# A fourth set of exp buffers, and third readings that ride in ScalarE-only PV steps

## The chip, the cores and the metric

The kernel runs on one core of one Trainium2 chip. The metric is the device time of one execution in microseconds; each number for a kernel is the median of several runs, all of them in the fast state.

## The reference, cut to what matters

One sequence of 2048 rows of 640 features goes through a layer norm. The result feeds an attention with 32 query heads of width 20 that share one key and one value head, and beside it a dense layer with SiLU. Everything is added to the input.

```
xn = _layernorm(x, axis=-1)
q = (xn @ wq) as 32 heads of 20;  k = xn @ wk;  v = xn @ wv        # one k, one v
p = softmax((q . k) * 20 ** -0.5);  o = p @ v
return x + o @ wo + silu(xn @ w1) @ w2
```

The exponentials are the mass: 32 heads x 2048 x 2048 scores, each of which must pass ScalarE or VectorE.

## The kernel before: the parts that matter

The program is written by a planner in Python: it keeps a model of each engine's clock, picks for each engine what runs next, and emits five fixed instruction lists tied by semaphores. The constants at its head (priorities, limits on backlog) steer the plan; a changed constant changes the order of instructions, not only their number.

Work goes in 688 steps. A step takes three heads ("units") and 128 keys: an S step makes the three score blocks (128 keys x 512 queries) in three PSUM banks; two such sets of banks alternate. ScalarE reads two or all three blocks with Exp. In a "dv" step VectorE takes the third block: it clamps it to integers (p1), whose bits, read as bf16, are a coarse exponential. Two shifted copies (Y) of the same bits make the second and third reading, whose weighted sum corrects the coarse one. The PV step multiplies the exponentials with V in four 32-wide column tiles of one PSUM bank: two heads of ScalarE, the first and the second reading of VectorE's head. The tiles are then full, so the third readings, collected over up to three dv steps, get a PV pass of their own.

```
NZ = 3          # sets of Z/Y buffers
ZB = 3          # dv steps that share a set
PV_PRESS = 12   # PV is urgent when more than NBLK - PV_PRESS = 19 exp blocks wait
DVE_TH = 3.0    # VectorE gets a block while its backlog is below this
U_PRIO = 0.9;  X_PRIO = 1.6     # p1 has 1.0; lower goes first
...
    def flush_z(self):               # after ZB dv steps (2 in the last two groups)
        zs = self.zset
        self.zset = (self.zset + 1) % NZ
        ...                          # two Y copies of the whole set on VectorE
        while ts and hosts and len(ts) % 3 == 1:
            ...                      # a lone third reading may ride in a ScalarE-only step
        while ts:
            part = ts[:3]            # else up to three make a pass of their own
            ts = ts[3:]
...
        # dummy products where PE would stand still
        if room < 0.08 or self.busy_share(now) > FILL_BELOW:
            return None
```

A set of Z/Y is written again NZ flushes later. Before that, all PV steps that read it must have run. The planner knows this, and orders every engine's list so that it holds.

The softmax here doesn't subtract the row's maximum and nothing guards it: scores larger than these inputs give would overflow.

## Time and profile before

| | before |
|---|---|
| time, median | 749.66 us (749.35 to 750.24, 4 runs) |
| span of the profiled run | 747.3 us |
| dv steps (VectorE blocks) | 603 of 688 |
| passes of third readings alone | 217, and no riders |
| dummy matmuls on PE | 147 (145 with a matmul record in the trace) |

The line is of the view of one source line; it gives the smallest, median and largest duration and then the first and last start.

```profile
L748 PEld LDWEIGHTS psall<-sbt x2048: 90/91/113, 16.4 to 734.2; 32*128 32x128 bf16 x187
```

The last score starts at 734.2 us; 13.1 us of the span are left for what comes after it.

### The profile page before, as it was taken

What the parts mean: (1) busy time and instruction counts of PE and PEld (TensorE: products, weight loads), DVE (VectorE), ACT (ScalarE), POOL (GpSimd) and SP (SyncE); (2) the same over time, 40 slices, a digit from 0 to 9 for tenths busy, and PEclk for the clock granted to TensorE, in tenths of its full rate; (3) what the DMA queues carried; (4) which work ended last, traced back from release to release, by engine and by line L of the source; (5) the groups of instructions that cost most, each with busy time, mean ns of one, the idle gap of its engine ahead of it and who ended that gap; (6) DMA issues with size and microseconds to landing.
All of it is one profiled execution on the core that took longest, in us unless ns stands there. A gap on an engine that the chain in (4) does not pass through costs nothing.

```text
span 747.3 us, 17758 instructions
## 1 busy us (share of the span) xinstructions
PE 713.0 (95%) x6724; PEld 230.7 (31%) x6779; DVE 709.2 (95%) x1390; ACT 709.3 (95%) x780; POOL 105.6 (14%) x280
## 2 busy tenths in 40 slices
PE   8889999999999999999999999999999999999996
PEld 4332222233323322223333332222333332223342
DVE  7889999999999999999999999999999999999987
ACT  7879999999999999999999999999999999999952
POOL 5421111010111111111011111101011100101100
PEclk9999999999999999999999999999999999999999
DMA  6570000000012211000002211000002110000011
GB/s 188 148 264 16 21 15 15 18 13 15 16 23 54 58 33 22 10 8 8 9 9 43 58 40 34 14 8 8 9 8 51 42 47 8 15 9 8 9 36 36
DMA packets 55962, 27.06 MB, mean 36 GB/s; under 512 B 43686, under 2 KB 55238, under 8 KB 55878
## 3 DMA queue, kind: packets, MB, share of 16 engines
q1 hardware_dynamic: 54566, 25.87, 13.4%
q8 instruction: 55, 0.90, 0.5%
q10 hardware_dynamic: 1312, 0.05, 0.1%
q14 instruction: 29, 0.24, 0.1%
HBM read 11.36 MB, written 2.62 MB: 19 GB/s over the span
## 4 chain that ended last, share of the span: by engine, by line
PE 51%; ACT 22%; DVE 15%; issue 6%; DMA 2%; POOL 2%; SPq 0%; DVEq 0%; ACTq 0%; POOLq 0%
ACT sbt L766 20%; PE psall L748 17%; PE psall L827 17%; PE psall L1112 8%; DVE sbt L780 7%; DVE sbt L839 4%; PE psall L1050 3%; ACT sbt L1058 3%; PE psall L1117 3%; DMA sbt<-sbt 2%; PE psall L1016 2%; PE psall L672 1%; DVE sbt L938 1%; DVE sbt L1023 0%; DVE sbt L1063 0%
## 5 line engine op out<-in xcount | busy, mean ns | idle before, releaser
L766 ACT ACTIVATE sbt<-psall 128x1024 bf16<-128x1024 f32 (+2 forms) x688 | 676.8, 1130 | 21.1 <-PE psall L748 15.7
L780 DVE TENSOR_SCALAR sbt<-psall 128x512 int16<-128x512 f32 x603 | 403.0, 683 | 15.0 <-PE psall L748 11.9
L748 PE MATMUL psall<-sbt 32*128 32x512 bf16 x2048 | 269.0, 385 | 14.1 <-ACT sbt L766 9.0
L827 PE MATMUL psall<-sbt 128*32 128x512 bf16 x3428 | 263.7, 384 | 1.7 <-DVE sbt L938 1.3
L839 DVE TENSOR_SCALAR sbt<-sbt 128x1536 int16<-128x1536 int16 (+2 forms) x434 | 220.0, 528 | 1.8
L748 PEld LDWEIGHTS psall<-sbt 32*128 32x128 bf16 x2048 | 68.7, 91 | 253.8 <-ACT sbt L766 123.6
L827 PEld LDWEIGHTS psall<-sbt 128*32 128x32 bf16 x3428 | 67.7, 94 | 111.5 <-issue 67.2
L908 POOL CAST sbt<-sbt 128x168 f32<-128x168 bf16 x42 | 15.2, 361 | 546.4 <-DMA sbt<-sbt 546.4
L1112 PE MATMUL psall<-sbt 128*128 128x320 bf16 x448 | 85.8, 302 | 0.1
L1050 PE MATMUL psall<-sbt 128*128 128x512 bf16 (+1 forms) x246 | 75.9, 384 | 4.6 <-issue 2.4
L1112 PEld LDWEIGHTS psall<-sbt 128*128 128x128 bf16 x448 | 34.8, 97 | 43.6 <-issue 33.0
L1063 DVE SCALAR_TENSOR_TENSOR sbt<-sbt,psall 128x512 bf16<-128x512 bf16 (+1 forms) x56 | 38.0, 679 | 3.1 <-PE psall L748 2.0
L1058 ACT ACTIVATE sbt<-psall 128x512 bf16<-128x512 f32 (+1 forms) x56 | 38.6, 689 | 0.0
L924 POOL TENSOR_TENSOR sbt<-sbt 128x240 bf16<-128x240 f32 (+2 forms) x44 | 26.7, 608 | 46.1 <-DVE sbt L915 46.1
L1117 PE MATMUL psall<-sbt 128*128 128x320 bf16 x160 | 31.3, 303 | 1.2 <-DVE sbt L1095 0.7
L1050 PEld LDWEIGHTS psall<-sbt 128*128 128x128 bf16 (+1 forms) x280 | 19.2, 98 | 41.5 <-issue 26.7
L938 DVE CAST sbt<-psall 128x512 bf16<-128x512 f32 x43 | 29.4, 683 | 1.4 <-PE psall L827 1.3
L910 POOL TENSOR_TENSOR sbt<-sbt 128x44 f32<-128x44 f32 x84 | 26.2, 312 | 6.6
L1016 PE MATMUL psall<-sbt 128*128 128x512 bf16 (+1 forms) x78 | 24.7, 384 | 2.3 <-issue 1.7
L672 PE MATMUL psall<-sbt 128*32 128x512 bf16 (+7 forms) x78 | 23.6, 353 | 0.0
L685 PE MATMUL psall<-sbt 128*128 128x512 bf16 (+4 forms) x67 | 18.2, 412 | 2.2 <-POOL sbt L1276 1.4
L1117 PEld LDWEIGHTS psall<-sbt 128*128 128x128 bf16 x160 | 12.1, 97 | 17.2 <-issue 9.7
(85 smaller groups left out, 198.6 us busy)
## 6 DMA issues: line engine op xcount, KB each, us to landing
sbt<-in_A_x_dram SPq DMA_DIRECT2D x32, 160.0 KB, 3.5
out_dram<-sbt SPq DMA_DIRECT2D x16, 160.0 KB, 1.8
sbt<-in_B_w_dram SPq DMA_DIRECT2D x5, 432.0 KB, 5.3
sbt<-sbt SPq DMA_DIRECT2D x105, 20.0 KB
sbt<-in_B_w_dram SPq DMA_DIRECT2D x13, 160.0 KB, 3.9
sbt<-sbt SPq DMA_TRANSPOSE x67, 2.4
sbt<-in_A_wo_dram SPq DMA_DIRECT2D x5, 160.0 KB, 6.2
sbt<-in_A_wq_dram SPq DMA_DIRECT2D x5, 140.0 KB, 3.7
```

Of the source, the lines that this page charges most:

```text
L748: ins = pe.matmul(self.bk(par3 + j), self.kT[r:r + SLOT, kk, kt * P:(kt + 1) * P], self.qT[r:r + SLOT, h // 4, (x // H) % 2, :], start=Tru ...
L766: return a.activation(self.E[:, b0 * QW:(b0 + na) * QW], self.ps[:, par3 * BANK:(par3 + na) * BANK], AF.Exp, scale=ACT_SCALE)
L780: return v.tensor_scalar(self.Z[:, zs, zp * QW:(zp + 1) * QW], self.bk(bb), 0.0, ZMAX, ALU.max, ALU.min)
L827: return pe.matmul(self.bk(UBANK, 0, QW, q * SLOT, (q + 1) * SLOT), self.v[:, w, kt, :], x, start=start, stop=stop, tile_position=(0, q * ...
L839: sc.new("dve", t_dve_4x(w), lambda v, k=k: v.tensor_scalar(self.Y[:, zs, k, 0:n * QW], Z, float(PH[k + 1][0]), None, ALU.add), zk, [("Y", ...
L938: return v.tensor_copy(self.U[0:rows, up, :], self.bk(UBANK, 0, QW, 0, rows))
L1016: return pe.matmul(self.bk(b, 0, QW, 0, rows), self.wq[:, k, lo:hi], self.xnT[:, k, c * QW:(c + 1) * QW], start=(k == 0), stop=(k == DC - 1))
L1050: return pe.matmul(self.bk(b, 0, QW, 0, rows), self.w1[:, k, fk * P:fk * P + rows], self.xnT[:, k, c * QW:(c + 1) * QW], start=(k == 0), s ...
L1058: sc.new("act", t_act(QW), lambda a: a.activation(t, src, AF.Tanh, scale=0.5), [("B", b)], [("tb", tp)], prio=X_PRIO, name=f"th{c}_{fk}")
L1063: sc.new("dve", t_dve_ps(QW), lambda v: v.scalar_tensor_tensor(out=self.hT[0:rows, fk, :], in0=t, scalar=1.0, in1=src, op0=ALU.add, op1=AL ...
L1112: return pe.matmul(self.bk(b, 0, 320), self.hT[0:rows, fk, i * P:(i + 1) * P], self.w2[0:rows, fk, e0:e0 + 320], start=(m == 0), stop=(m = ...
L1117: return pe.matmul(self.bk(b, 0, 320), self.oT[:, k, i * P:(i + 1) * P], self.wo[:, k, e0:e0 + 320], start=(m == 0), stop=(m == tot - 1))
```

## The change

Its intent: free enough memory for a fourth Z/Y set, so that a set may stay in use for longer, and use that freedom to carry third readings over from flush to flush. A step in which ScalarE takes all three heads leaves the fourth column tile free, and such a step can now take one third reading along. Five constants are tuned anew.

```diff
-NZ = 3
+NZ = 4
-PV_PRESS = 12
-DVE_TH = 3.0
-U_PRIO = 0.9
-X_PRIO = 1.6
+PV_PRESS = 8
+DVE_TH = 3.2
+U_PRIO = 1.1
+X_PRIO = 0.8
-DVE_FROM = 10
+DVE_FROM = 8
@@ memory
-        self.wqp = sb([P, DC, 2 * P], BF16)       # now inside oT
-        self.kv_st = sb([P, 2, DC, DH], BF16)     # now inside U
-        self.wk = sb([P, DC, P], BF16)            # now inside ost
-        self.o = sb([P, 2, 4, D], BF16)
+        self.o = sb([P, 4, D], BF16)
@@ do_S: a new ScalarE-only step takes a carried reading
+        if self.thirds and self.can_host(pv):
+            self.host(pv, self.thirds.pop(0))
@@ flush_z
-        while ts and hosts and len(ts) % 3 == 1:
-            ...
-        while ts:
-            part = ts[:3]
-            ts = ts[3:]
+            if seen and self.can_host(op) and ts:
+                self.host(op, ts.pop())
+        ...
+        self.thirds += ts
+        while len(self.thirds) >= 3 or (end and self.thirds):
+            part = self.thirds[:3]
+            self.thirds = self.thirds[3:]
```

(Cut, besides what `...` stands for: the helpers can_host and host, keys of the dependence tracking for the shared memory, one rule on banks for the v products in the start, the index c % 2 that goes with the second o buffer.)

More of the change, by code (lines that the diff above doesn't have):

```diff
@@ L379, in alloc @@
         self.U = sb([P, 2, QW], BF16)
+        self.kv_st = self.U[:, 1, 0:2 * DC * DH].rearrange("p (a c d) -> p a c d", a=2, c=DC)
         self.stk = sb([P, 64], BF16)
@@ L383, in alloc @@
         self.hT = sb([P, FC, QW], BF16)
-        self.o = sb([P, 2, 4, D], BF16)
+        self.o = sb([P, 4, D], BF16)
         self.oT = sb([P, DC, QW], BF16)
+        self.wqp = self.oT[:, :, :].rearrange("p c e -> p (c e)")[:, 0:DC * 2 * P].rearrange("p (c e) -> p c e", c=DC)
         self.tb = sb([P, 2, QW], BF16)
@@ L390, in alloc @@
         self.ost = sb([P, 3, D], BF16)
+        self.wk = self.ost[:, 2, :].rearrange("p (c e) -> p c e", c=DC)
         self.idf = self.w2[:, 4, 0:2 * P].bitcast(F32)
@@ L406, in alloc @@
         hflat = self.hT[:, :, :].rearrange("p a b -> p (a b)")
-        oflat = self.o[:, :, :, :].rearrange("p a b c -> p (a b c)")
-        self.okeys = [("o", a, h) for a in range(2) for h in range(H)]
+        oflat = self.o[:, :, :].rearrange("p b c -> p (b c)")
+        self.okeys = [("o", h) for h in range(H)]
         def xslot(n):
@@ L414, in xslot @@
                 return self.xres[:, n - self.XS, :]
-            return oflat[:, DC * D:(DC + 1) * D]
+            return oflat[:, 3 * D:4 * D]
         def xkeys(n):
@@ L459, in steps_init @@
         self.nqd = 0
+        self.thirds = []
         self.y_done = {}
@@ L475, in more, with bank_for_job @@
                 or self.cur_job is not None)
-    def bank_for_job(self):
-        if not self.started:
+    def bank_for_job(self, job=None):
+        if not self.started and (job is None or job.name[0] != "v"):
             banks = [7, 6, 5, 4, 3]
@@ L514, in job_ready @@
             return INF
-        return max(r, self.bank_for_job()[0])
+        return max(r, self.bank_for_job(job)[0])
     def s_reads(self, t, dv):
@@ L633, in step @@
                 job = cand.popleft()
-                job.bank = self.bank_for_job()[1]
+                job.bank = self.bank_for_job(job)[1]
                 self.cur_job = job
@@ L857, in flush_z @@
         first = self.zblocks[0][1]
-        tail = None
-        if self.pv_wait[-1][0].kt == KT - 1:
-            tail = self.pv_wait.pop()
+        end = self.pv_wait[-1][0].kt == KT - 1
+        tail = self.pv_wait.pop() if end else None
         seen = False
-        hosts = []
         for op, _ in self.pv_wait:
             seen = seen or op is first
-            if seen and op.after is not None and not op.after and op.kt < KT:
-                hosts.append(op)
-        while ts and hosts and len(ts) % 3 == 1:
-            th, key, kt = ts.pop()
-            op = hosts.pop()
-            op.after.append(th)
-            op.mm += 1
-            op.deps |= sc.deps_of([key], ())
-            sc.readers[key].append(op)
-        while ts:
-            part = ts[:3]
-            ts = ts[3:]
+            if seen and self.can_host(op) and ts:
+                self.host(op, ts.pop())
+        if end and self.can_host(tail[0]) and len(self.thirds + ts) % 3 == 1:
+            self.host(tail[0], ts.pop() if ts else self.thirds.pop())
+        self.thirds += ts
+        while len(self.thirds) >= 3 or (end and self.thirds):
+            part = self.thirds[:3]
+            self.thirds = self.thirds[3:]
             def fn(pe, part=part):
@@ L884, in flush_z @@
             op.mm = len(part) + len(part) // 3
-            op.kt = part[-1][2]
+            op.kt = max(x[2] for x in part)
             op.na = 0
@@ L891, in flush_z, with can_host, host @@
         self.zblocks = []
+    def can_host(self, op):
+        return op.after is not None and not op.after and op.kt < KT
+    def host(self, op, third):
+        th, key, kt = third
+        op.after.append(th)
+        op.mm += 1
+        op.deps |= self.sc.deps_of([key], ())
+        self.sc.readers[key].append(op)
     def norm_dma(self, g, rows):
@@ L919, in norm_dma @@
             h0, m = us[js[0]] % H, len(js)
-            dst = self.o[:, c % 2, :, h0 * DH:(h0 + m) * DH].rearrange("p q (i d) -> p q i d", d=DH)
+            dst = self.o[:, :, h0 * DH:(h0 + m) * DH].rearrange("p q (i d) -> p q i d", d=DH)
             src = w[:, :, js[0]:js[0] + m, 0:DH]
@@ L924, in norm_dma @@
             sc.new("pool", 0.15 + 4 * m * DH * 0.00186, lambda v, dst=dst, src=src, rb=rb: v.tensor_tensor(
-                dst, src, rb, ALU.mult), [("W", 0), ("W", 1), ("rL", up)], [("o", c % 2, h0 + i) for i in range(m)],
+                dst, src, rb, ALU.mult), [("W", 0), ("W", 1), ("rL", up)], [("o", h0 + i) for i in range(m)],
                 prio=0.5, name=f"nrm{g}").lock = True
@@ L974, in end_group @@
                 m = len(rq)
-                dst = self.o[:, c % 2, :, hh * DH:(hh + m) * DH].rearrange("p q (i d) -> p q i d", d=DH)
+                dst = self.o[:, :, hh * DH:(hh + m) * DH].rearrange("p q (i d) -> p q i d", d=DH)
                 src = xv[:, :, rq[0]:rq[0] + m, 0:DH]
@@ L979, in end_group @@
                 op.after.append(sc.new("dve", t_dve_ps(4 * m * DH), lambda v, dst=dst, src=src, rb=rb: v.tensor_tensor(
-                    dst, src, rb, ALU.mult), [("UB",), ("rL", up)], [("o", c % 2, hh + i) for i in range(m)],
+                    dst, src, rb, ALU.mult), [("UB",), ("rL", up)], [("o", hh + i) for i in range(m)],
                     prio=U_PRIO, name=f"nrm{g}"))
@@ L1005, in consume @@
                        [("B", b), ("offq",)], ks, prio=X_PRIO, name=f"qev0_{ht}")
-        reads = [("xnT", i) for i in range(4)] + [("wq", ht)]
+        reads = [("xnT", i) for i in range(4)] + [("wq", ht)] + [("oT", i) for i in range(4)]
         return Job(f"q0_{ht}", mms, reads, consume, width=QW)
@@ L1077, in try_oT @@
             op = self.sc.dma("sp", lambda q, i=i: q.dma_start_transpose(
-                self.oT[:, 0:nk, i * P:(i + 1) * P], self.o[:, c % 2, i, 0:nk * P]),
-                [("o", c % 2, h) for h in range(need)], [("oT", i), ("oTv", c, i)], nk * P * P * 2,
+                self.oT[:, 0:nk, i * P:(i + 1) * P], self.o[:, i, 0:nk * P]),
+                [("o", h) for h in range(need)], [("oT", i), ("oTv", c, i)], nk * P * P * 2,
                 sem=self.s_oT[i], name="oTd")
@@ L1089, in f @@
             def f(pe, b, i=i):
-                return pe.transpose(self.bk16(b)[:, i * P:(i + 1) * P], self.o[:, c % 2, i, k * P:(k + 1) * P],
+                return pe.transpose(self.bk16(b)[:, i * P:(i + 1) * P], self.o[:, i, k * P:(k + 1) * P],
                                     self.idb[:, :])
@@ L1096, in consume @@
                    [("B", b)], [("oT", i) for i in range(4)] + [("oTl",)], prio=X_PRIO, name="oTl")
-        reads = [("o", c % 2, h) for h in range(H)] + [("idb",)]
+        reads = [("o", h) for h in range(H)] + [("idb",)]
         return Job("oTl", mms, reads, consume, gate=lambda: self.norm_made[c] == H)
@@ L1277, in prologue @@
         pool(0.1, lambda g: g.memset(self.eps[:, :], EPS), [], [("eps",)])
-        pool(0.7, lambda g: g.memset(self.wk[:, :, :], 0.0), [], [("wk",)])
+        pool(0.7, lambda g: g.memset(self.wk[:, :, :], 0.0), [], [("wk",), ("ost", 2, 0), ("ost", 2, 1)])
         wqd = self.wqp[:, :, :].rearrange("p c (h j) -> p c h j", j=SLOT)
@@ L1281, in prologue @@
         for kk in range(2):
-            pool(0.4, lambda g, kk=kk: g.memset(wqd[:, :, 4 * kk:4 * kk + 4, DH:SLOT], 0.0), [], [("wq", kk)])
+            pool(0.4, lambda g, kk=kk: g.memset(wqd[:, :, 4 * kk:4 * kk + 4, DH:SLOT], 0.0), [],
+                 [("wq", kk)] + [("oT", i) for i in range(4)])
         iv = self.idf[:, :].rearrange("p (r j) -> p r j", j=SLOT)[:, :, DH:DH + 2]
@@ L1313, in wkrep @@
             s = self.kv_st[:, 0, :, :]
-            src = bass.AP(self.kv_st, s.offset, [list(s.ap[0]), list(s.ap[1]), [0, 4], [1, DH]])
+            src = bass.AP(self.U, s.offset, [list(s.ap[0]), list(s.ap[1]), [0, 4], [1, DH]])
             return a.activation(dst, src, AF.Copy)
@@ L1350, in mvk @@
             return [("mv", n) for n in range(a, b_)]
-        oflat = self.o[:, :, :, :].rearrange("p a b c -> p (a b c)")
+        oflat = self.o[:, :, :].rearrange("p b c -> p (b c)")
         def xa(n):
@@ L1434, in prologue @@
                     self.qT[:, ht, par, :], self.zero[:, 0:QW], self.offq[:, :], None, ALU.add),
-                    [("zero",), ("offq",)], [("qb", par, h) for h in range(4 * ht, 4 * ht + 4)],
+                    [("zero",), ("offq",), ("mv", 3)], [("qb", par, h) for h in range(4 * ht, 4 * ht + 4)],
                     prio=6.0 + par, name="qz")
@@ L1479, in consume @@
                                                                  ALU.mult), [("wo",)], [("wo",)], prio=2.0)
-            return Job(f"kv{j}", mms, [("xnT", 2 * j), ("xnT", 2 * j + 1), ("wk",)], consume)
+            return Job(f"kv{j}", mms, [("xnT", 2 * j), ("xnT", 2 * j + 1), ("wk",), ("ost", 2, 0), ("ost", 2, 1)], consume)
         def v_job(n0, n1):
```

## The prediction

> **What bounds the kernel now.** I read the page's first two parts for busy shares, the groups by shape for what one piece costs, the windows for where idle time lies, the timeline for start-to-start costs, and the waits for who holds whom.
>
> ```profile
> PE 713.0 (95%) x6724; PEld 230.7 (31%) x6779; DVE 709.2 (95%) x1390; ACT 709.3 (95%) x780; POOL 105.6 (14%) x280
> ```
>
> Three engines stand at 95%, so no share names the bound. The windows (sums of PE, PEld, DVE, ACT, POOL, then clock, DMA share, GB/s) part them:
>
> ```profile
> 300.00:400.00 100.00, 96.35 (x933) 30.61 (x931) 94.22 (x176) 99.90 (x109) 10.89 (x28) 1.00 0.05 9
> 600.00:700.00 100.00, 96.58 (x913) 29.24 (x919) 97.91 (x183) 99.99 (x112) 10.67 (x30) 1.00 0.07 16
> 700.00:720.00 20.00, 20.00 (x190) 7.59 (x183) 17.26 (x38) 15.07 (x19) 1.75 (x5) 1.00 0.18 35
> 720.00:735.00 15.00, 14.91 (x116) 5.66 (x115) 13.74 (x32) 8.00 (x13) 1.93 (x5) 1.00 0.05 10
> ```
>
> From 60 to 700 us ScalarE has no idle time to speak of, VectorE has a few per cent, and PE looks full. In the last two windows ScalarE starves and PE is full. PE's fullness in the middle is partly make-believe: the schedule fills PE's pauses with dummy products.
>
> ```profile
> L672 PE MATMUL psall<-sbt 128*32 128x512 bf16 (+7 forms) x78 | 23.6, 353 | 0.0
> L685 PE MATMUL psall<-sbt 128*128 128x512 bf16 (+4 forms) x67 | 18.2, 412 | 2.2 <-POOL sbt L1276 1.4 <-DVE sbt L1496 0.5 <-issue 0.2
> ```
>
> Those 145 instructions (41.8 us, some in the start) do no work; a PE that has room for them is not the bound in the middle. So I take the middle as bound by ScalarE, whose load depends on how many exp blocks VectorE takes from it, and the tail from 700 us on as bound by PE with VectorE close behind.
>
> ```profile
> L766 ACT ACTIVATE sbt<-psall 128x1024 bf16<-128x1024 f32 x591 | 565.1, 1090 | 11.7 <-PE psall L748 6.4 <-PE psall L827 4.9
> L780 DVE TENSOR_SCALAR sbt<-psall 128x512 int16<-128x512 f32 x603 | 403.0, 683 | 15.0 <-PE psall L748 11.9
> L827 PE MATMUL psall<-sbt 128*32 128x512 bf16 x3428 | 263.7, 384 | 1.7 <-DVE sbt L938 1.3
> L839 DVE TENSOR_SCALAR sbt<-sbt 128x1536 int16<-128x1536 int16 x346 | 188.9, 559 | 1.7
> L766 ACT ACTIVATE sbt<-psall 128x1536 bf16<-128x1536 f32 x83 | 124.1, 1503 | 0.8 <-PE psall L748 0.8
> ```
>
> There are 688 steps: one S step makes the scores of three heads (two in the last 16). In 603 of them VectorE takes one head (L780, then two added readings, L839) and ScalarE two; in 83 ScalarE takes all three. Mean durations overlap, so I take costs from start to start:
>
> ```profile
> 319.87 4.76 ACT L766 ACTIVATE sbt<-psall 128x1024 bf16<-128x1024 f32 x5
> 324.48 0.65 ACT L1058 ACTIVATE sbt<-psall 128x512 bf16<-128x512 f32 x1
> 324.95 5.18 ACT L766 ACTIVATE sbt<-psall 128x1536 bf16<-128x1536 f32 x5
> 329.97 0.66 ACT L1058 ACTIVATE sbt<-psall 128x512 bf16<-128x512 f32 x1
> ```
>
> Five two-head exps: (324.48-319.87)/5 = 0.92 us, some with a small wait; the trace's commonest distance is 0.904. The second five hold one three-head exp, 5.02-4x0.92 = 1.34 (commonest distance 1.330). A step moved to VectorE therefore frees ScalarE of 0.426 us. On VectorE the commonest distances are 0.600 for L780 and 0.465 for a 1536-wide L839, so a block costs 0.600+2x0.465/3 = 0.91 us.
>
> **What the Trainium skill says.** "Perfetto Trace Analysis", section "Optimizing Scalar/DVE Operations", says a profiled instruction's latency holds a write-acknowledgement that overlaps with the next one; the trace agrees (1090 ns mean against 904 from start to start), which is why I don't use means. "TensorEngine Tiling (Array Packing)", section "Key Properties", says tiles work independently and a change of tiling mode drains the array. The trace agrees with the first: 20 PV matmuls of about 385 ns stand in 1.26 us at 325.13, five passes of four at (1.26-0.39)/4 = 0.22 us. So PV work is counted in passes, not in matmuls, and a matmul in an empty column tile is free. "Perfetto Trace Analysis", section "Identifying Performance Opportunities", says consistent bubbles can mean that buffers ran out. The middle shows hardly any on ScalarE; VectorE's L780 idles 15.0 us, 11.9 of it released by scores (L748), not by a PV pass that frees an exp buffer. This is my ground for expecting little of the fourth buffer by itself.
>
> **The change, part by part.**
>
> Memory: a fourth Z and Y set costs 3x512x2+2x3x512x2 = 9216 bytes per partition. Aliasing gives wqp 2560, kv_st 400, wk 1280 and one of two o halves 5120 = 9360. It just fits. No time of its own.
>
> Third readings: every VectorE block has a third reading that needs a fourth-and-more column tile. Before, each flush made its own pass for them. Flushes: 346/2 = 173 of three blocks and, from the other forms of L839 (x80 and x8), 40 of two and 4 of one; 173x3+80+4 = 603. Up to 217 passes. Matmul count confirms it: 589 full VectorE steps x4 + 83x3 + last group 47 = 2652, plus 173x4+80+4 = 776, equals the 3428 of L827; so at most the four singles ever rode along. After, each of the 83 ScalarE-only steps can host one, except those before the first VectorE block of their group (about 20, most in the first group), so some 60; the 540 left are carried over flushes and packed in threes, with a remainder at each of 43 group ends. With about 14 blocks per group, 1.5 hosted, 4.5 passes: about 190. That saves some 27 to 30 passes, 30x0.22 = 6.6 us of PE, plus mode changes. In the middle this mostly turns into dummies or pauses: worth 0 to 1 us through scores that come a little sooner. In the tail, flushes of two blocks are forced in the last two groups (14 passes for 28 blocks before, about 10 after); PE is full there, so 4x0.22 = 0.9 us counts.
>
> More VectorE blocks: starting at step 8 instead of 10 admits up to 2; the backlog limit of 3.2 instead of 3.0 us, and fewer reuse waits, let VectorE idle less. VectorE is busy 94 to 98 in 100 us; over 60 to 700 us its idle time is about 17 us by busy union. Filling half of that is 8.5/0.91 = 9 more blocks (603 to about 612), which takes 9x0.426 = 3.8 us from ScalarE, the bound. This is the largest term, and the half is my choice.
>
> PV pressure 12 to 8: PV may lag up to 23 instead of 19 exp blocks; other jobs go first. Worth smoothing, not work; at the end up to 4 blocks more of PV are left, 1 to 2 passes = +0.3 us.
>
> Priorities: evictions of the other products (0.8) now go ahead of L780 (1.0), and the accumulator's eviction (1.1) behind it. It moves 0.4 to 0.7 us of VectorE time before or after a score's reading; net unknown, I put 0 with +-2 us.
>
> One o buffer: writes of the next chunk's normalised heads wait for four transposes of the chunk before (1.2 us each to issue, 2.4 to land, about 7 us), three times, on POOL, which is 14% busy: 0. In the start, aliases and fewer banks for v jobs: 0 to +1 us.
>
> Sum: -3.8 (blocks) -0.5 (scores sooner) -0.9 +0.3 (tail) +0.4 (start) = -4.5 us: 749.5-4.5 = 745.0 us.
>
> **Rivals.** First, PE as the bound throughout: the chain of waits gives it 51%, and PE's busy row is full. Then all 30 passes count with their mode changes, about 0.3 us each, 9 us, and with the blocks -13: 737 us. Against it speak the 145 dummies and ScalarE's 99.9%. Second, VectorE takes over: scores wait for it already.
>
> ```profile
> PEld psall L748 <- ACT sbt L766: 123.6, 320, 1.5
> PEld psall L748 <- DVE sbt L780: 35.3, 85, 0.8
> PEld psall L748 <- DVE sbt L839: 16.3, 41, 0.5
> ```
>
> The scores wait 2.4 times as long for ScalarE as for these two lines. If longer backlogs and evictions set ahead raise the VectorE waits by half, 26 us, and a tenth of it reaches ScalarE, the gain of the blocks is nearly eaten: 748 to 750 us. Third, the block count does not move, since a limit on backlog is a level and not a rate: then only tail and start are left, 749 us. Fourth, the new write-after-read wait on o reaches PE through late output products: three times up to 7 us of delay, but the jobs are spread over a chunk of some 180 us, so I give it little.
>
> **Range and chances.** Rival one sets the low side (737, with some more blocks 735), rivals two and three the high side (750). I choose 737.5 to 750.0. Faster by over 2% needs less than 734.8 us: all three engines would have to come near 97% over the whole span; 0.05. Slower by over 2% means 764 us; nothing here costs 15 us; 0.01. Within 2%: 0.94.
>
> **What would show it.** L766's 1536-wide count falls and L780's rises by equal numbers, about 9 (right) or under 3 (third rival). Of L827, passes fall by about 30, seen in fewer matmuls: each replaced pass of three saves one matmul, so the count less four per added block falls by tens. Dummies (L672, L685) should grow if PE was not the bound and stay if it was. ScalarE stays over 99% busy in the middle windows and VectorE rises to about 98. Waits of L748 on L780 tell of rival two. The prediction is wrong if ScalarE's idle time in the middle grows, if the start lengthens by more than 2 us, or if the tail after 700 us changes by more than 2 us.

## The result, and the profile after

The changed kernel takes 745.34 us (744.68 to 747.35, 4 runs), the kernel before 749.66 us. The ratio is 0.9946, interval 0.9925 to 0.9967. A ratio here is the mean time of one kernel's runs over that of the other's of the same rounds, so it isn't quite the ratio of the medians. The predicted 745.0 us is nearly exact. Whether the reasons are right is another matter; the rest of this document is about that.

The groups of the changed kernel by shape, in the order in which the prediction showed them (L767 answers to L766, L781 to L780, L830 to L827, L842 to L839), and the dummies (L673, L686):

```profile
L767 ACT ACTIVATE sbt<-psall 128x1024 bf16<-128x1024 f32 x596 | 569.8, 1080 | 11.5 <-PE psall L749 10.5 <-PE psall L830 0.6
L781 DVE TENSOR_SCALAR sbt<-psall 128x512 int16<-128x512 f32 x608 | 406.4, 684 | 16.5 <-PE psall L749 10.2 <-PE psall L830 3.4
L830 PE MATMUL psall<-sbt 128*32 128x512 bf16 x3434 | 264.7, 387 | 0.0
L767 ACT ACTIVATE sbt<-psall 128x1536 bf16<-128x1536 f32 x78 | 116.1, 1493 | 3.6 <-PE psall L830 2.4 <-PE psall L749 1.1
L673 PE MATMUL psall<-sbt 128*32 128x512 bf16 (+9 forms) x86 | 26.6, 389 | 0.0
L686 PE MATMUL psall<-sbt 128*128 128x512 bf16 (+2 forms) x57 | 14.3, 406 | 1.4 <-POOL sbt L1283 1.4
```

VectorE took 5 blocks more (603 to 608) and ScalarE's three-head exps fell by the same 5 (83 to 78). The PV matmuls rose by 6. The program's own lists say why: 60 third readings ride, and 193 passes are left (169 of three, 17 of two, 7 of one) where 217 stood. Dummies went from 147 to 143.

The profile's first part seems to say that PE became busier, by 8 us:

```profile
PE 721.1 (97%) x6781; PEld 230.5 (31%) x6781; DVE 713.9 (96%) x1397; ACT 707.9 (95%) x780; POOL 111.7 (15%) x280
```

It did not. The Trainium skill, "Perfetto Trace Analysis", section "Identifying the Most-Contended Engine", warns that matmul busy time is a bad measure of how near a kernel is to its limit; here it is bad for one more reason. In the kernel before, one dense product (L1050) has 246 matmul records but 280 weight loads; after, both are 280. All in all 53 dense matmuls lack a record in the trace before and none in that after, and 53 x 0.22 us (such matmuls mostly follow each other at 0.216 or 0.226 us in these traces) is 11.7 us of busy time that only the records lack. This is an estimate; by it PE was busy some 3.6 us less than before.

Where the time went is told better by when the same score starts in both traces (after minus before, from the starts of the S matmuls): -3.2 us at step 20, +3.8 at step 100, +1.1 at step 650, -1.9 at the last step. So in this profiled pair the changed kernel wins in the first 20 steps, loses 7 us by step 100, wins back 2.7 us in the long middle and 3 us in the last two groups. (The profiled run of the changed kernel is the slowest of its four, 747.35 us: the two profiled spans lie 1.7 us apart, the medians 4.3.)

### The profile page after: what moved, and what is told of

Same layout as the page of the kernel before. It is cut to its first block, busy times and chain, and to the rows that moved or that the text cites. A ratio compares the mean times of both kernels' runs of the same rounds, so it can differ in the third digit from the quotient of the medians.

```text
span 745.6 us, 17784 instructions
## 1 busy us (share of the span) xinstructions
PE 721.1 (97%) x6781; PEld 230.5 (31%) x6781; DVE 713.9 (96%) x1397; ACT 707.9 (95%) x780; POOL 111.7 (15%) x280
## 4 chain that ended last, share of the span: by engine, by line
PE 51%; DVE 20%; ACT 19%; issue 5%; POOL 2%; DMA 2%; DVEq 0%; ACTq 0%; POOLq 0%; SPq 0%
ACT sbt L767 18%; PE psall L830 17%; PE psall L749 17%; DVE sbt L781 9%; PE psall L1057 6%; PE psall L1119 5%; DVE sbt L842 5%; PE psall L1023 2%; PE psall L1124 2%; PE psall L673 2%; DVE sbt L1070 1%; DMA sbt<-sbt 1%; ACT sbt L1065 1%; DVE sbt L945 1%; DVE sbt L1352 1%
## 5 line engine op out<-in xcount | busy, mean ns | idle before, releaser
L767 ACT ACTIVATE sbt<-psall 128x1024 bf16<-128x1024 f32 (+2 forms) x688 | 674.4, 1117 | 21.7 <-PE psall L749 18.1
L781 DVE TENSOR_SCALAR sbt<-psall 128x512 int16<-128x512 f32 x608 | 406.4, 684 | 16.5 <-PE psall L749 10.2
L749 PE MATMUL psall<-sbt 32*128 32x512 bf16 x2048 | 269.5, 385 | 12.0 <-ACT sbt L767 6.0
L830 PE MATMUL psall<-sbt 128*32 128x512 bf16 x3434 | 264.7, 387 | 0.0
L842 DVE TENSOR_SCALAR sbt<-sbt 128x1536 int16<-128x1536 int16 (+2 forms) x436 | 223.9, 533 | 1.5
L749 PEld LDWEIGHTS psall<-sbt 32*128 32x128 bf16 x2048 | 69.7, 91 | 252.8 <-issue 86.8
L830 PEld LDWEIGHTS psall<-sbt 128*32 128x32 bf16 x3434 | 67.2, 95 | 112.4 <-issue 75.1
L915 POOL CAST sbt<-sbt 128x168 f32<-128x168 bf16 x42 | 17.3, 411 | 522.0 <-DMA sbt<-sbt 522.0
L1119 PE MATMUL psall<-sbt 128*128 128x320 bf16 x448 | 86.8, 303 | 0.0
L1057 PE MATMUL psall<-sbt 128*128 128x512 bf16 (+1 forms) x280 | 83.6, 384 | 1.6 <-DVE sbt L1070 1.0
L1119 PEld LDWEIGHTS psall<-sbt 128*128 128x128 bf16 x448 | 34.0, 97 | 43.4 <-issue 34.8
L1057 PEld LDWEIGHTS psall<-sbt 128*128 128x128 bf16 (+1 forms) x280 | 19.6, 98 | 41.3 <-issue 23.3
L1023 PE MATMUL psall<-sbt 128*128 128x512 bf16 (+1 forms) x95 | 28.4, 385 | 0.0
L673 PE MATMUL psall<-sbt 128*32 128x512 bf16 (+9 forms) x86 | 26.6, 389 | 0.0
L912 POOL TENSOR_TENSOR sbt<-sbt 128x84 f32<-128x84 bf16 x42 | 18.0, 429 | 0.0
L1124 PEld LDWEIGHTS psall<-sbt 128*128 128x128 bf16 x160 | 12.0, 97 | 16.6 <-issue 11.7
```

What stands on the lines that cost most here:

```text
L673: return pe.matmul(self.bk(UBANK, 0, n, 0, 32), self.zero[:, 0:32], self.zero[:, 0:n], start=False, stop=False, tile_position=(0, 0), skip ...
L749: ins = pe.matmul(self.bk(par3 + j), self.kT[r:r + SLOT, kk, kt * P:(kt + 1) * P], self.qT[r:r + SLOT, h // 4, (x // H) % 2, :], start=Tru ...
L767: return a.activation(self.E[:, b0 * QW:(b0 + na) * QW], self.ps[:, par3 * BANK:(par3 + na) * BANK], AF.Exp, scale=ACT_SCALE)
L781: return v.tensor_scalar(self.Z[:, zs, zp * QW:(zp + 1) * QW], self.bk(bb), 0.0, ZMAX, ALU.max, ALU.min)
L830: return pe.matmul(self.bk(UBANK, 0, QW, q * SLOT, (q + 1) * SLOT), self.v[:, w, kt, :], x, start=start, stop=stop, tile_position=(0, q * ...
L842: sc.new("dve", t_dve_4x(w), lambda v, k=k: v.tensor_scalar(self.Y[:, zs, k, 0:n * QW], Z, float(PH[k + 1][0]), None, ALU.add), zk, [("Y", ...
```

## The experiments

All runs below give correct results. All times are medians, from five rounds beside the kernel before (749.41 to 749.71 us); the row "after" has the four runs of the result.

| run | sets | tuning | carry and ride | time, us | ratio to before, 95% |
|---|---|---|---|---|---|
| before | 3 | old | no | 749.66 | 1 |
| merged_only | 3 | old | no | 751.69 | 1.0022 (1.0010 to 1.0034) |
| four_sets_old_tuning | 4 | old | no | 746.73 | 0.9967 (0.9948 to 0.9985) |
| carry_old_tuning | 4 | old | yes | 749.87 | 1.0004 (0.9993 to 1.0016) |
| after_no_carry | 4 | new | no | 746.41 | 0.9961 (0.9949 to 0.9973) |
| after | 4 | new | yes | 745.34 | 0.9946 (0.9925 to 0.9967) |
| after_three_sets | 3 | new | yes | 761.72 | 1.0158 (1.0145 to 1.0171) |
| after_three_sets_press12 | 3 | new, PV_PRESS 12 | yes | 752.95 | 1.0039 (1.0026 to 1.0052) |

My theory from the prediction was that time goes by the number of VectorE blocks and that the fourth set by itself gives little. The rivals: the fourth set is the gain; or PE is the bound and the saved passes are.

### One part at a time

**merged_only**: the aliased buffers, one o buffer and the rule on banks in the start; everything else as before.

```diff
 NZ = 3                       # changed kernel, back to three sets, old constants,
                              # flush_z and do_S as before; the aliases stay
```

> The aliased scratch buffers alone: three Z/Y sets, the old tuning, third readings flushed as before. The plan holds 605 VectorE blocks (603 before) and 217 third-reading passes (as before). All theories agree that sharing memory is nearly free: 749.7 us within 1 us; two blocks more would be 0.9 us less by the ScalarE price of 0.426 us. If it is over 751 us, the aliases cost time in the start and the rest of the change has to pay that back.

It took 751.69 us, 2.0 us more than before. The aliases are not quite free. The start isn't the cause: its scores keep within 2.1 us of those of the kernel before to step 650, with no lasting lag before step 500. The POOL wait that the prediction foresaw for the single o buffer is there, some 7 us at a time as worked out:

```profile
POOL sbt L935 <- DMA sbt<-sbt: 14.9, 2, 8.2
```

(POOL's normalising multiply waits for the transposes of the chunk before: 14.9 us in two waits, the longest 8.2.) These two waits end at 229 and 409 us, and the scores lag by only 0.1 us at steps 300 and 400, so they don't hold up the scores there. In this trace the lag opens late, from 0.7 us at step 660 to 5.7 at step 668, and 1.6 us are left at the end. Whether the 2 us come from the aliases as such, or from the new order with 605 blocks in place of 603, no run separates.

**four_sets_old_tuning**: the same with the fourth set.

```diff
-NZ = 3                       # against merged_only
+NZ = 4
```

> Aliases and the fourth set, old tuning, no carrying and no riding: 600 VectorE blocks, 217 passes. Theory of the prediction (time goes by the number of VectorE blocks, the buffer alone gives little): 3 blocks fewer, so 749.7+1.3 = 751 us. Rival (the fourth set itself lets scores be read without waiting for a PV pass that frees a set): faster than before although it has fewer blocks, 746 us or less. Rival PE: no pass is saved, so 749.7.

746.73 us, with 600 blocks, five fewer than merged_only. By my theory this kernel had to be the slower one. It is faster, by 5.0 us of the medians and by 4.1 us if the ratios are divided (0.9967/1.0022 = 0.9945); the intervals are apart. The theory that blocks carry the gain has fallen. (The profiled run of this kernel is the slowest of its six, 749.56 us, and so a poor picture of the gain: its span is only 1.4 us shorter than that of merged_only, 747.4 against 748.8 us.)

**after_three_sets**: the changed kernel without its fourth set.

```diff
-NZ = 4                       # against the changed kernel
+NZ = 3
```

> The changed kernel with three sets in place of four, all else kept: 611 VectorE blocks (608 with four), 194 passes and 58 riders. Theory of the prediction: 3 blocks more, 745.3-1.3 = 744 us, within 2 us. Rival of the fourth set: slower than the kernel before, 755 us or more, since thirds are carried over and PV may lag more, so a set is held longer; VectorE's score readings (L781) then wait for PV passes (L830) for 10 us or more, against 3.4 us with four.

761.72 us, 16.4 us slower than with four sets and 12 us slower than the kernel before, although it has 611 blocks, three more. Here one sees where buffers that run out take their time. From 100 to 700 us (columns: length, then busy time of PE, PEld, DVE, ACT, POOL, clock, DMA share, GB/s), first three sets:

```profile
100.00:700.00 600.00, 588.53 (x5599) 185.08 (x5596) 575.43 (x1072) 584.76 (x630) 73.80 (x182) 1.00 0.10 23
```

then the changed kernel with four:

```profile
100.00:700.00 600.00, 592.09 (x5665) 182.80 (x5668) 586.90 (x1094) 598.53 (x645) 78.88 (x187) 1.00 0.10 23
```

ScalarE is busy for 584.76 us with three sets and 598.53 us with four: of the 15.6 us between these two profiled runs, 13.8 are ScalarE standing idle in the middle. The waits of the three-set kernel (total, times, longest):

```profile
ACT sbt L767 <- PE psall L749: 34.1, 39, 2.7
...
DVE sbt L781 <- PE psall L830: 8.2, 11, 1.9
```

and of the changed kernel:

```profile
ACT sbt L767 <- PE psall L749: 18.1, 19, 3.0
...
DVE sbt L781 <- PE psall L830: 3.4, 2, 2.1
```

The direct mark of the shortage, p1 (L781) waiting for the PV pass that frees its set (L830), grew by only 4.8 us, to 8.2 where the rival had put 10 or more. The larger part stands under another name: ScalarE waits for scores (L749), 16.0 us more. A reading of these lines that fits, though no run tests its middle link: p1 that can't write leaves its PSUM bank full, the score two steps on can't start, and ScalarE starves.

**after_no_carry**: four sets and new tuning, but third readings flushed as before (the lines of flush_z and do_S shown in the change, set back).

> The changed kernel without carrying and riding, so every flush makes its own passes as before: four sets and the new tuning stay; 607 VectorE blocks (608), 219 passes (193). Rival PE (every pass counts): 26 passes at 0.22 to 0.3 us, 745.3+5.7 to 7.8 = 751 to 753 us. Theory of the prediction: 0.4 us for one block and 1 us in the tail, 746.7 us. Rival of the fourth set: 745 to 747 us.

746.41 us, 1.1 us above the changed kernel, with overlapping intervals. It fell where my theory and the rival of the fourth set both put it, and far from the 751 to 753 us that 26 passes more would cost if every pass counted. Carrying and riding, the cleverest part of the change, is worth about 1 us, and even that isn't sure.

**carry_old_tuning**: four sets, carrying and riding, all five constants old.

```diff
-PV_PRESS = 8                 # against the changed kernel; also DVE_TH 3.0,
+PV_PRESS = 12                # U_PRIO 0.9, X_PRIO 1.6, DVE_FROM 10
```

> The changed kernel with all five tuning constants set back: four sets, carrying and riding under the old tuning. 599 VectorE blocks (608), 183 passes (193), 69 riders. It completes the square with four_sets_old_tuning (746.7 us), after_no_carry (746.4) and after (745.3). Theory that the fourth set is the gain and the other two parts are each worth about 1 us: 745.5 to 747.5 us. Rival (carrying needs the new tuning, since a carried reading holds a set longer and PV must be allowed to lag): 749 us or more.

749.87 us: the rival had the number right. Its reason isn't shown: in this trace the list of waits has no line in which p1 waits for a PV pass, and from 60 to 700 us ScalarE is busy for 637.69 of 640 us, against 636.30 in four_sets_old_tuning. With old constants carrying costs 3.1 us against four_sets_old_tuning (intervals apart), though it has 34 passes fewer (183 against 217). The new constants are worth 4.5 us with carrying and 0.3 us without. So the parts don't add: the fourth set pays alone, the new tuning pays only with carrying, and carrying costs time under the old tuning and gains 1 us at best under the new. Why, stays open.

**after_three_sets_press12**: is it the lag of PV that wants the fourth set?

```diff
-NZ = 4                       # against the changed kernel
+NZ = 3
-PV_PRESS = 8
+PV_PRESS = 12
```

> The changed kernel with three sets and the old PV pressure of 12, so that PV may lag 19 exp blocks again and not 23: 611 VectorE blocks, 189 passes. Lag theory (three sets cost 16 us since a set stays in use until its PV steps have run, and the new pressure lets these run later): half or more of the 16 us come back, 750 to 754 us, and ScalarE's wait for scores, 34.1 us with three sets and pressure 8, falls below 25 us. Rival (it is the carrying that holds the sets, not the lag): 758 us or more.

752.95 us: 8.8 of the 16.4 us came back. ScalarE's wait for scores fell to

```profile
ACT sbt L767 <- PE psall L749: 25.4, 27, 2.9
```

and just missed the expectation of below 25. A lower lag limit heals half of the shortage; the other half (7.6 us) this run leaves. Carrying, which holds a set until its last third reading has run, is one candidate, but it need not be the main one: with the old tuning and no carrying at all, three sets already cost 5.0 us against four (merged_only against four_sets_old_tuning). Three sets with the new tuning but without carrying were not tried.

### Where the fourth set pays under the old tuning

The scores of merged_only and four_sets_old_tuning stay within 2.9 us of each other to step 660, where they are 0.5 us apart; at step 671 the four-set kernel is 5.3 us ahead. In the last two groups flushes are of two blocks, so three sets hold six blocks and not nine. I took the tail for the place. But of this lead only 1.4 us are left where the two spans end, so this pair of traces doesn't hold the 5.0 us that I looked for in it. What it does show in these groups is ScalarE waiting for scores, in merged_only

```profile
ACT sbt L767 <- PE psall L749: 17.7, 21, 2.8
```

and in four_sets_old_tuning

```profile
ACT sbt L767 <- PE psall L749: 11.8, 16, 1.9
```

over the whole run. The difference lies after 700 us: 12.5 against 5.7 us there.

**four_sets_last_two_groups**: three sets, and four in the last two groups only.

```diff
-        self.zset = (self.zset + 1) % NZ
+        self.zset = (self.zset + 1) % (4 if self.zblocks[0][0] // KT >= self.NG - 2 else 3)
```

> As merged_only (751.7 us; three sets, old tuning, no carrying), but the fourth set is used in the last two groups alone, where flushes are of two blocks and sets turn over faster. 604 VectorE blocks. Tail theory (with the old tuning the fourth set pays only where flushes are short; the traces of merged_only and four_sets_old_tuning run level to step 660 and part by 5 us after it): 746.5 to 748 us. Rival (it pays everywhere, a little in each group): over 750 us.

749.62 us: 2.1 of the 5.0 us. Its interval overlaps that of merged_only by a little and is apart from that of four_sets_old_tuning. My tail theory accounts for less than half, and the rival's bound of 750 us wasn't met either. Where the rest sits stays open; I did not run the opposite case.

**before_tail_flush3**: the kernel before, with flushes of three to the very end.

```diff
-len(self.zblocks) >= (ZB if g < self.NG - 2 else 2)
+len(self.zblocks) >= ZB
```

> The kernel before with one threshold changed: the last two groups flush three blocks at a time like all others, so three sets hold nine blocks there and not six. No fourth set, no merged memory. 601 VectorE blocks, 212 third-reading passes (217). Tail theory: it gains like the fourth set did, 745 to 747 us. Rival (short flushes keep the end short, and what the fourth set gave in the tail was something else): 749 us or slower.

748.44 us, 1.0 us less than before (interval 0.9976 to 0.9999), where I expected 2.5 to 4.5 us. What is striking is that its last score starts 7 us sooner than in the kernel before (727.1 against 734.2 us) and it finishes 1 us sooner. Scores that end early are not the end. The next run says what is.

### What a PE pass costs

**after_pack_two**: the changed kernel with third readings packed in twos, 277 passes in place of 193.

```diff
-        while len(self.thirds) >= 3 or (end and self.thirds):
-            part = self.thirds[:3]
-            self.thirds = self.thirds[3:]
+        while len(self.thirds) >= 2 or (end and self.thirds):
+            part = self.thirds[:2]
+            self.thirds = self.thirds[2:]
```

> A dose test of PE passes: the changed kernel with third readings packed in twos instead of threes: 277 passes of their own (193), 607 VectorE blocks, 109 dummy instructions (143). Theory that PE has room in the middle: 84 passes at 0.22 us = 18.5 us of PE work are mostly taken from dummies and pauses, below +8 us, and that mostly in the tail: 746 to 753 us. Rival PE (every pass counts, with mode changes up to 0.3 us): 764 to 770 us.

757.56 us, 12.2 us more for 84 passes: 0.145 us a pass, where a pass takes 0.22. Both theories fell; the truth lies between. The groups of PV and dummies in this run:

```profile
L830 PE MATMUL psall<-sbt 128*32 128x512 bf16 x3263 | 283.5, 384 | 3.5 <-DVE sbt L945 2.2 <-DVE sbt L1479 0.5 <-DVE sbt L1504 0.4
...
L673 PE MATMUL psall<-sbt 128*32 128x512 bf16 (+9 forms) x51 | 14.5, 354 | 0.0
```

PV took 283.5-264.7 = 18.8 us more of PE, and the dummies of L673 gave up 26.6-14.5 = 12.1 (those of L686 took 0.7 more). So much the pauses could take. And yet the middle did not slow down at all: the last score starts at 723.4 us here,

```profile
L749 PEld LDWEIGHTS psall<-sbt x2048: 90/91/112, 15.6 to 723.4; 32*128 32x128 bf16 x187
```

and in the changed kernel at 732.2:

```profile
L749 PEld LDWEIGHTS psall<-sbt x2048: 90/91/100, 15.3 to 732.2; 32*128 32x128 bf16 x187
```

Of these 8.8 us, 5.0 stand at step 100 already, where the changed kernel's profiled run had lost time; from there to step 650 this run gains 1.0 us more.

The price is paid after the last score, 32.0 us in this run and 13.4 in the changed kernel. The window from 735 to 748 us, first this run, then the changed kernel:

```profile
735.00:748.00 13.00, 13.00 (x90) 8.32 (x91) 5.78 (x12) 0.00 (x0) 0.00 (x0) 1.00 0.00 1
```

```profile
735.00:748.00 13.00, 4.69 (x39) 2.62 (x33) 6.78 (x17) 0.00 (x0) 0.00 (x0) 0.90 0.14 50
```

With twos, PE is full for the whole 13 us while ScalarE has nothing left to do: the dense products, displaced from the middle, are done there. The trace shows the displacement for the output products of line L1119, here from 100 to 700 us and from 700 us on (PE, PEld, clock, DMA share, GB/s), first in this run:

```profile
100.00:700.00 600.00, 65.65 (x336) 25.66 (x336) 1.00 0.10 23
700.00:756.00 56.00, 17.14 (x112) 10.19 (x112) 0.97 0.11 27
```

then in the changed kernel:

```profile
100.00:700.00 600.00, 78.71 (x406) 30.84 (x406) 1.00 0.10 23
700.00:756.00 56.00, 8.10 (x42) 3.19 (x42) 0.98 0.13 27
```

Seventy of them moved from the middle to the end, and with them 15 of L1057. At 0.14 and 0.22 us from start to start, as most follow each other in these traces, that is some 13 us, an estimate close to the 12.2 us that the run lost.

This is what a busy share of 95% on three engines meant. In the middle ScalarE sets the pace of the scores. But the dense products must fit into PE's gaps, and what doesn't fit is carried to the end, where PE alone sets the time.

**after_few_dummies**: dummies only below a busy share of 0.65.

```diff
-FILL_BELOW = 0.78
+FILL_BELOW = 0.65
```

> The changed kernel with dummy products only where PE's busy share is below 0.65 and not 0.78: 76 dummies and not 143, 606 VectorE blocks, 196 passes. Theory that dummies stand in true pauses: PE's idle time grows by what they took, some 18 us, and the time stays within 1.5 us of 745.3 unless the clock is halved more often. Rival (they take time from real work): 743 us or less at a clock of 0.993 or more.

744.10 us, the lowest median (ratio 0.9928, interval 0.9916 to 0.9940): clear of the kernel before, while its interval overlaps that of the changed kernel (0.9925 to 0.9967). Its dummies:

```profile
L686 PE MATMUL psall<-sbt 128*128 128x512 bf16 (+3 forms) x49 | 13.4, 427 | 1.8 <-POOL sbt L1283 1.4 <-issue 0.2 <-DVE sbt L781 0.2
L673 PE MATMUL psall<-sbt 128*32 128x512 bf16 (+6 forms) x25 | 8.1, 410 | 0.0
```

They fell from 40.9 to 21.5 us, and the time by 1.2. So nearly all of the 19.4 us seems to have stood in true pauses, as the theory said, though the plan changed with it (196 passes, 606 blocks). The clock didn't fall for it (0.991 to 0.995, the changed kernel's 0.991 to 0.993).

**after_tail_flush3**: the tail's threshold of three, in the changed kernel, as a try for something better.

```diff
-len(self.zblocks) >= (ZB if g < self.NG - 2 else 2)
+len(self.zblocks) >= ZB
```

> A try for a version that beats both: the changed kernel with flushes of three blocks in the last two groups too, which gave the kernel before 1.0 us. 604 VectorE blocks, 191 passes. If the tail is bound by PE's whole work (after_pack_two ended its scores 8.9 us sooner than the changed kernel and finished 10 us later), sooner scores alone give nothing: 744.5 to 746 us. If scores that end sooner shorten the end, 742 to 744 us.

744.97 us (ratio 0.9935, 0.9923 to 0.9947): as the first case had it. The last score starts at 722.0 us, 10 us before that of the changed kernel, and the time follows by 0.4 us in the medians (3.8 in the profiled pair, whose changed kernel is a slow one). The same lesson a third time.

### A run that did not test its theory

**after_warm_start**: dummies up to a busy share of 0.97 before step 40.

```diff
-        if room < 0.08 or self.busy_share(now) > FILL_BELOW:
+        if room < 0.08 or self.busy_share(now) > (0.97 if self.s_next < 40 else FILL_BELOW):
```

> The changed kernel with more dummy products before step 40 (their limit on PE's busy share goes from 0.78 to 0.97 there), so that PE's clock is not halved in the start: 168 dummy instructions (143), 609 VectorE blocks. Clock theory: the changed kernel's profile shows half clock for 6.8+3.4+3.4 us in the start against 3.4 us in the kernel before, and its lead of 3.2 us at step 20 is a lag of 1.7 us at step 30; with a warm clock some 3 us come back: 741.5 to 743 us and a mean clock of 0.995 or more. Rival (the dummies delay the real work as much as the clock did): 745 to 747 us.

747.48 us, 2.1 us slower than the changed kernel by the medians, though the intervals still overlap (0.9959 to 0.9983 against 0.9925 to 0.9967). The clock was still halved, for 6.8 us from 37.9 us on, so the run doesn't say what the clock costs, and that these dummies cost time is likely but not shown. Against the clock as an explanation speak the runs of the kernel before: three at a mean clock of 1.000 took 749.31, 749.53 and 749.80 us, others at 0.995 took 748.89, 749.72 and 749.75. The changed kernel's own runs lean the other way, with 747.35 us at 0.991 and 744.68 to 745.82 at 0.993, while after_few_dummies took 743.94 at 0.991. What made the changed kernel lose 7 us between steps 20 and 100 in its profiled run, where after_no_carry, after_few_dummies and after_tail_flush3 lose 3 to 5, stays open. Its clock was halved for 13.6 us of the first 60 there, theirs for 3.4 to 6.8 us, which would fit but isn't a test.

## Why the prediction was right, and where it wasn't

The time was right, 745.0 against 745.34 us. Its largest term, 3.8 of 4.5 us, was not, so that the number came out is largely luck.

- **What bounds the kernel**: ScalarE bounds the middle (busy for 598.5 of 600 us after), and PE the end: both held. "A PE that has room for them is not the bound in the middle" held for the scores and failed for the whole: 84 passes more cost two thirds of their length, at the end. Neither I nor the first rival had the displaced dense products.
- **"My ground for expecting little of the fourth buffer by itself"**: this is the step that failed. I took the absence of a wait on PV in L780's line for the absence of a shortage. The set is worth 5.0 us under the old tuning and 16.4 under the new with carrying. In the traces of merged_only and four_sets_old_tuning the list of waits, down to 0.2 us, has no line in which p1 waits for PV, and still the medians lie 5 us apart. What these lists do show is ScalarE's wait for scores, 17.7 us with three sets and 11.8 with four. So the shortage need not appear under the name of the buffer, and what the buffer is worth only a run with more of them shows.
- **More VectorE blocks**: the price per block (0.426 us) wasn't tested; the count was 5, not 9, so the term would be 2.1 us, not 3.8. The windows give 18.7 us of VectorE idle time from 60 to 700 us, not the 17 that the prediction read, and 14.0 after: a quarter was filled and not a half, 4.7 us, about what 5 blocks at 0.91 need. The runs don't obey it in any case: four_sets_old_tuning with 600 blocks beats merged_only with 605, and after_three_sets with 611 is the slowest of all.
- **Third readings**: 24 passes saved against 27 to 30 expected; the gain of about 1 us was what I put, and carrying costs 3.1 us under the old tuning, which I did not see. The sign I gave for it, a count of L827 that falls by tens after four per added block are taken off, was wrong: such a block adds two matmuls and not four, its second and its third reading, so of the 3434 ten come off and 3424 are left, 4 fewer than before. The passes of two went from 40 to 17, and those cost no extra matmul; of the passes of three only 4 went.
- **Other signs**: dummies were to grow if PE was not the bound and to stay if it was; they stayed (147 and 143), though PE does not set the pace in the middle, so the sign was a poor one. Rival two's sign came: the scores' waits for L780 and L839 rose from 51.6 to 73.4 us (L781 and L842 after). It did no harm in the middle, where ScalarE's idle time fell from 2.6 to 2.2 us between 60 and 700 us.
- **Priorities, 0 within 2 us**: the five constants together gave 0.3 us without carrying and 4.5 us with it.
- **Memory and start**: "no time of its own" was 2.0 us for the aliases, or for the new plan that came with them. The start's +0.4 us was +3.8 at step 100 in the profiled run, though within 0.3 us of 0 in three other kernels with four sets and the new tuning (after_no_carry, after_few_dummies, after_tail_flush3).
- **Tail**: -0.6 us was about -3 us in the profiled pair. Both this and the start are beyond the limits that I had set myself under what would make the prediction wrong.

So the number came out because terms that were wrong in opposite directions cancelled. By runs, with each part added in turn: aliases +2.0, fourth set -5.0, tuning -0.3, carrying and riding -1.1, together -4.3 us before rounding. In another order, with carrying before the tuning, the last two are +3.1 and -4.5.

## What to carry to other kernels

In a kernel whose instruction order is fixed beforehand, test a buffer count by running with one more and one fewer, since the profile of the given count need not name the shortage. Retune after a structural change, and judge the change and the tuning together: here, with four sets, the new tuning alone was worth 0.3 us and carrying alone cost 3.1. And where several engines stand near 95%, look at what happens after the last piece of the pacing stream: work that seemed hidden may only have been put off.

## What the Trainium skill lacked or had wrong

- "Perfetto Trace Analysis", section "Identifying Performance Opportunities", gives consistent bubbles on the engine that should be saturated as a possible sign of too few buffers. Not wrong: with three sets in the changed kernel ScalarE does stand idle. But it doesn't say that the semaphore waited for can be another than the buffer's: the wait that names the shortage is 8.2 us against 3.4 us, while the loss is 16.4 us, most of it under the wait for scores (34.1 against 18.1 us).
- The same page, section "Identifying the Most-Contended Engine", warns of matmul busy time because of pipelining. It doesn't say that matmul records can be missing: 246 records beside 280 weight loads for one product here, 53 in all, which makes PE look 11.7 us less busy.
- "TensorE: Matmul & The Clock Gate", section "Terms", puts the penalty of a throttle at its time times (1 - K/N). By that rule a mean clock of 0.995 costs 749 x 0.005 = 3.7 us. In the kernel before no such penalty shows between a mean clock of 1.000 (749.31 to 749.80 us) and 0.995 (748.89 to 749.75 us). These runs have no trace, so whether the halved time lay where PE had nothing urgent to do isn't known.
- No page has the price of work on an engine that isn't the bound but must finish: here 0.145 us for a pass of 0.22 us.
